# Chunk bounds by min/max trees, keys of eight heads in one DMA transpose, and a new instruction order

## The chip, the cores and the metric

The kernel runs on one core of a Trainium2 chip. The metric is the device time of one execution in microseconds (us); lower is better. The engines are named as the profile names them: PE (TensorE matmul; PEld its weight loads), DVE (VectorE), ACT (ScalarE), POOL (GpSimd), and SP, which here only issues DMAs. A name with a q (SPq) is an engine's instruction queue.

## The reference

Two stages. First a sparse causal attention over 4 batches, 8 heads, 768 positions and head size 64: every query keeps its 6 best chunks of 32 keys, ranked by an upper bound that comes from the minimum and maximum of each chunk. Then an MLP with an ELU over the 3072 tokens.

```python
k_min, k_max = min and max of k over each chunk of 32 keys       # 24 chunks per head
ub = sum over d of max(q*k_min, q*k_max), causal by chunk
top_chunks = argsort(ub)[..., -6:]
attn = softmax(where(key's chunk in top_chunks and key <= query, q @ k.T / 8, -1e9)) @ v
x = attn.transpose(0, 2, 1, 3).reshape(3072, 512)
h = x @ w_in                                                     # 512 -> 2048
out = where(h > 0, h, exp(min(h, 0)) - 1) @ w_out                # 2048 -> 512
```

## The kernel before

**Units.** The queries are cut into eight units of 384 tokens: unit 0 and unit 1 take the first half of batches 0 and 1 together (names with `p` and `s`), units 2 to 7 take batch and half (0,1), (1,1), (2,0), (2,1), (3,0), (3,1). For each unit the kernel prepares keys and queries (`prep_pair`, `prep`), selects chunks (`select`), attends (`attend_pair`, `attend`) and then runs the MLP (`mlp`). Below, H2 stands for one of the 16 first-layer blocks of unit 2 (L829, four matmuls of 128x384) and O2.1 for a quarter of token tile 1 of its second layer (L850, four matmuls of 128x512). The MLP of a unit is laid between the score (`sc`, L760) and value (`pv`, L811) matmuls of the next unit's attention on PE.

**Chunk bounds.** For batches 0 and 1 the bounds are reduced from transposed keys in PSUM (L362). For batches 2 and 3 `bounds_batch` loads the keys a second time with a chunk to each partition: 96 partitions (4 heads, 24 chunks), 32 keys of 64 numbers, in two loads of 16 keys (`kc`, one buffer). Each load gets two `tensor_reduce` on DVE, minimum and maximum (L481, out 96x64 from 96x1024 f32, read with a stride). Two small joins (`kj`, L485), a subtraction (`kz`), a PE transpose (`kw`, L492) and four copies (`kv`) bring the result to `kst`, which `select`'s matmul `ub` (L578) reads.

**Keys of batches 2 and 3.** `keys` casts 128 keys of eight heads into a `kt` buffer (`kb`), puts a one-hot row of the chunk beside them (`ky`), and SP issues two DMA transposes (`kd`, L463), one for heads 0 to 3 and one for heads 4 to 7, each 128x512 in bf16, into that group's own `lhs` buffer.

**From attention to the MLP.** The value matmuls of a head pair are followed by `rcp` (L622) and `on` (L624) on DVE, and for units 2 and up by a DMA transpose `xd` (L635) from SP. The first H block of a unit needs all four transposes of its unit.

**Order.** Nothing is scheduled at run time. A graph of operations is built, and a written-out string gives, three characters at a time, the engine and the operation; each engine runs its own instructions in the order of the string, and a second string gives the buffer slot of each new buffer. So an instruction that waits holds everything that stands behind it on its engine, and SP's and POOL's DMA issues wait in line as well. `fill` (L889) is a matmul on zeros that computes nothing.

Of the kernel before, what the change touches and what calls it, by code (L numbers as in the profile page):

```python
# [9 lines left out]
AOT = mybir.AluOpType  # L10
# [7 lines left out]
S = 768  # L18
D = 64
# [20 lines left out]
G0hD0nD01D00D0iD0jD0cG0eD06A0rS0tS0vS0xS0sS0uS0wS0yS0VS0WS0XS0YS0zS0BG0kG03G04D05PjNPjOPjPPjQPjR  # L40
P0DD09G0pG0lG0aG0bG0dD0oA02P0KA0LA0HP0MA0QP1oD0FD0ED0qP1uD0OD0ND0RP0TA0UP1kP1yP1jP1lA1mA1nG0mG0g
P11D13A15D12G0JP1pP1aD1ePjSPjTPjUPjVPjWP1hP18P1tP1qS0ZS0+S2fS2gS2hD0GD1iP1zA19P1vA1sA0IA1xA1wA10
G07G16S2iD1bG1gG0PG1fG0fG0AGmrGmsGmtD0CPjXPjYPjZPj-Pj+P1OP1AA1BGmuGmvGmwD0-P1DD1cP1EP1HP1SD1FP1I
G1dD1JP1RD1TD1GPk0Pk1Pk2Pk3P2oD1UP1ND2pD1KP2BD1PD1QD2DA1CP20P1YP1+D21D2qP1LA1rP1XP25P2aP29P26D22
D1ZD2bA2FA2sG2uG08D1-D2CD27G14S2IS2OS2vS2PS2QA1MA2HP1VA1WD28D2cS2RS2kPk4Pk5Pk6Pk7Pk8Pk9PkaPkbP23
PkcPkdPkePkfPkgPkhP2dD2eA24PmCA2GA17PkiPkjPkkPklP2wPmGP2JA2KD2MPkmPknPkoPmOPm-A2xA2LD2yG2rG2jGmx
D2NAmDAmHAm+G2SG2EP3lD3mD3nD3pD3oD2AAbeA0SA2zGmIDmEDmJDmFGn0D3qDn1D2tPmSPmWPmKPmyAmLAmXAmPGmYGmQ
D3rDmZD3uAmTDmUDmRDmVGmMPnuPnaPnmA3vP4FPn2AnvA3tA3sAnnGnwGnoDmNDnxDnpP41P4DPneAn3AmzA4GA4EAnbGn4
Dn5A42P4jA4kAnfP2XP3JP3HPniS32S5wS2mS2TS50S4+S2VS3fGmADncD2+DndPn6A3IAn7DmBPnLGngD2YD2ZDnhG2-G4H
Gn8P4lA3KG3LA4mA30P38PnqPnMPnED39Dn9AnrDnsD3aD3cD4nD3bG3dG31PnFP3+PnNAnjDnkDnlDntP3gP33PnGA34A36  # L50
G37G2lD3hG3jG3kG2nD3iA40G43D35P3wPnyPnOAnPD3ePnHS4ZD3xD3yD3zD3AD3BP3NA2UAnID3CG3DD3ES8hS4-S4YS7Q
S7US4XP4JP3MD3OP48P45P44D46P3QP4aA49A4bP4IA3RD3GD47D4cD4KPnzP3SP4OG3FP4uG2WP4eP4dP4sPnAD3PD4fD4g
D4LP4MA3TG3UP3WA4vA4tA4PP3VP4hA4ND4wP4xP4pP4yD3XD3YD4zP4oP3ZA3-P5fA5gG5iA5jP5rA5sP5ED4QG7RS7KS7O
ScMP4SP4RD4qD4AD4rD4iPnBD5FA5GD4TD4UP4BA4CP5xDnCP4VP5QP58D5uD5yA5BG5DG5IG5CA4WPoxP5JD5hD59D5zA5R
A5TD5SAoyGozG5HPo9AoaGobA5NA5tD5cD5aP5kD5mPodAoePnVAnWA7PGofG5UD5bDocD5lA5oDogDoAPohPo5Ao6S51G52
Go7G5ADnXPnZPnRPotD5LD5KDnYDo8ShqS55S7SS7IG5eG5nAnSGnTDnUA5vAouPo1Ao2An-GovDowD5MGo3Do4AoiSnKS57
S7NSazS7LGn+PoFA56AoGGojDo0PolAomPoBDokGoHDoIP5VD5WPoRPopPoXPoSPoYPp2Pp3G5pGonDooD5XAoqG5qGorAoC
GoDA5PD5YD5ZD5-D5+D60G5dP6gA62DoEA6hP6lP68A69P6mP6cA6dA6nDosPoTD7TSnJS53SnDS7JScKSaFDaHS7MSnQDaG
P66A67P6aP6iA6jD6kG61A6bPp4P6uA6vP6GA6HP6eA6fD6oG54PoJP6yP64A65A6zP6wA6xPoZAoKP6IP6LP6MP6pP6AA6J
A6BP6qDoLDoMP6CA6NG63G5OP7uP6EPoND6rD6sP74SaIA6DG6KA7vA6FAoOGoPSaBS6tA75P6YA6ZD6OP6PP79P7aP6QA7b  # L60
DaKDoQDbaDaMP76A77G78D6RPoUDaJP7AP7wA7xP70P7zD6SDaLDaNA71Pp5Dp6A7BP6UP6-P6WA6VP8cA6XS6TSp7SaTA6+
AoVPo-P7oP72P7sA73P7iP7mA7pA7nG7cP7dD8dG8fG8gG7CD7yDo+Sp1Sp0P7eP7kP7qP8iD7fD7gS7hA7jA7tA7rP85P7V
P8uP7DD8jD8eD7ZD7XA7lP7ED7FD7GD7+A7-A8ySayA8AP8BP8pA8qG8sS7HA89G8bA8CA8ED8mD8vD8wD8nP80A81A8aAaC
A8zA84AaAD86D7WD7YD87G8xG8oD8rD8DD88Db6ScOSaDPpsPpEPpgA82SaxSavSoWD8kDfMD8lGcNDaEAphG83GpiApFGpG
DpHPp8PpwPpAPpoAptAcLDpjGpuG8FDpvSatSauScEApBGpCDpDApxAcPGpyDpzAppGpqPpcApdAbdSbgDprPpIPpkDcRGpe
DpfAp9GpaDpbApJGpKAplGpmDpLPpMApNA8tP8GD8IPpQSffSfhPpYPq4PpUAq5DpnPq8PqkGpOGb5Sb8ScGSbfApRGq6GpS
Gb9SbcD8KD8HD8JSawSbbShoApZPq0Aq1ApVDpTD8LD8MA8PPq9PqlDpPPqmDq7D8QGp-Dp+Dq2Dq3G8NP91A92P8ZPafAag
A8-D8OGpWDpXPqaP93A94G95P97P8RA8SP9tP96P9rP8VA9uA98P8XA8YPqbP8TP8+A9sA90PbmPqnDcYDqcScJSb7ScFDcQ
# [870 lines left out]
```

## Time and profile before

| | before |
|---|---|
| time, median of 3 runs | 303.69 us (300.88 to 304.95) |
| the profiled execution | 303.33 us, of it the span in the profile 301.6 us |
| busy: PE, DVE, ACT, POOL | 273.8, 230.6, 205.6, 127.7 us |
| mean granted TensorE clock | 0.983 |
| `fill` matmuls run | 40 |
| instructions | 6849 |

Busy time is the union of an engine's instructions. In views by windows each row is a stretch of the span: its length, then the busy time of each engine with the number of its instructions that start there, the clock granted to PE (1.00 is full), the busy share of the DMA engines and what they moved. In rows of the timeline the first number is the start, the second the duration, and the brackets hold how long the engine had been idle and what ended that.

### The profile page before, as it was taken

The numbers are of one execution on the slowest core, as the hardware profiler recorded it, in microseconds if no ns is written. First come the engines' busy times: TensorE is split into PE (matmuls) and PEld (weight loads), VectorE is DVE, ScalarE is ACT, GpSimd is POOL, SyncE is SP. The second block draws the span as 40 slices with busy tenths as digits, with TensorE's granted clock in tenths as the row PEclk, the third lists the DMA queues.
The fourth block names the chain that finished last, engine by engine and source line by source line (L and its number), as shares of the span: only waits on it lengthen the run. The fifth ranks groups of instructions, "written<-read, shape, count | busy, mean of one in ns | idle before, by whom it ended". The sixth has DMA issues, their size and how long they took to land.

```text
span 301.6 us, 6849 instructions
## 1 busy us (share of the span) xinstructions
PE 273.8 (91%) x2408; PEld 164.6 (55%) x2436; DVE 230.6 (76%) x622; ACT 205.6 (68%) x455; POOL 127.7 (42%) x254
## 2 busy tenths in 40 slices
PE   6779799999996879999699889999969999999994
PEld 4456454775464745567256446567535646665641
DVE  5673989799989878858899989784998679622740
ACT  3556792878496877689368929977766959891720
POOL 8862356448533357531366404402444515400510
PEclk9999999999999979999689999999999999999999
DMA  6999999999750599999697424823420230013002
GB/s 157 193 181 206 199 206 183 214 215 220 181 152 20 171 240 153 181 257 143 147 205 157 105 56 103 175 55 93 129 42 4 62 96 0 27 38 110 24 0 105
DMA packets 107347, 39.25 MB, mean 130 GB/s; under 512 B 98864, under 2 KB 102960, under 8 KB 107312
## 3 DMA queue, kind: packets, MB, share of 16 engines
q1 hardware_dynamic: 103216, 34.52, 56.3%
q0 software_dynamic: 3696, 4.19, 8.0%
q8 instruction: 19, 0.31, 0.5%
q14 instruction: 16, 0.13, 0.2%
q10 hardware_dynamic: 400, 0.10, 0.1%
HBM read 30.41 MB, written 6.29 MB: 122 GB/s over the span
## 4 chain that ended last, share of the span: by engine, by line
PE 50%; DVE 25%; DMA 11%; ACT 5%; issue 4%; POOL 2%; SPq 1%; POOLq 0%; ACTq 0%; DVEq 0%
PE bank L850 17%; PE bank L829 14%; DVE km L481 9%; PE bank L760 6%; DVE gT L842 5%; PE bank L811 4%; DMA kc<-in_k_dram 4%; DMA xt<-on 3%; DMA f<-in_v_dram 2%; PE bank L578 2%; DVE on L624 2%; PE bank L397 2%; ACT e L836 1%; DVE thr L597 1%; PE bank L529 1%
## 5 line engine op out<-in xcount | busy, mean ns | idle before, releaser
L829 PE MATMUL bank<-xt,w_in_sb 128*128 128x384 bf16 x512 | 95.4, 336 | 8.6 <-DMA xt<-on 4.6
L850 PE MATMUL bank<-w_out_sb,gT 128*128 128x512 bf16 x357 | 89.3, 379 | 2.3 <-DVE gT L842 0.7
L838 POOL TENSOR_SCALAR m<-e 128x384 f32<-128x384 f32 x96 | 49.2, 525 | 80.4 <-ACT e L836 67.0
L836 ACT ACTIVATE e<-bank 128x384 f32<-128x384 f32 x128 | 58.2, 491 | 28.5 <-PE bank L829 24.5
L829 PEld LDWEIGHTS <-w_in_sb 128*128 128x128 bf16 x512 | 50.8, 100 | 46.3 <-issue 17.3
L775 ACT ACTIVATE pt<-bank 128x384 bf16<-128x384 f32 (+1 forms) x144 | 66.5, 544 | 7.7 <-PE bank L760 5.9
L842 DVE SCALAR_TENSOR_TENSOR gT<-bank,m 128x384 bf16<-128x384 f32 x128 | 65.9, 549 | 4.9 <-POOL m L838 3.5
L850 PEld LDWEIGHTS <-gT 128*128 128x128 bf16 x384 | 36.1, 97 | 39.6 <-DVE gT L842 2.7
L760 PE MATMUL bank<-rhs,lhs 96*128 96x384 bf16 (+2 forms) x240 | 42.7, 293 | 1.8 <-DVE on L624 1.7
L792 POOL TENSOR_TENSOR pt<-pt,tri 128x256 bf16<-128x256 bf16 (+1 forms) x23 | 20.1, 884 | 31.7 <-ACT pt L779 18.0
L481 DVE TENSOR_REDUCE km<-kc 96x64 f32<-96x1024 f32 x16 | 30.3, 1909 | 2.4 <-DMA kc<-in_k_dram 2.3
L760 PEld LDWEIGHTS <-lhs 96*128 96x128 bf16 x240 | 21.4, 97 | 13.8 <-issue 0.5
L316 POOL CAST rhs<-qt 64x384 bf16<-64x384 f32 x26 | 13.7, 530 | 27.8 <-DVE qt L316 15.4
L811 PE MATMUL bank<-vext,pt 128*128 128x65 bf16 x576 | 23.2, 193 | 1.5 <-DVE pt L792 1.2
L811 PEld LDWEIGHTS <-pt 128*128 128x128 bf16 x576 | 21.5, 97 | 5.2 <-DVE pt L792 1.9
L314 ACT ACTIVATE o<-bank 128x512 f32<-128x512 f32 x12 | 7.2, 596 | 23.8 <-PE bank L850 23.6
L624 DVE TENSOR_TENSOR on<-bank,rcp 128x384 bf16<-128x384 f32 (+1 forms) x40 | 19.7, 500 | 1.1
L362 DVE TENSOR_REDUCE kst<-bank 128x12 f32<-128x384 f32 x32 | 16.9, 547 | 3.8 <-ACT kt L314 2.5
L622 DVE RECIPROCAL rcp<-bank 128x6 f32<-128x6 f32 (+1 forms) x40 | 7.2, 185 | 14.7 <-PE bank L811 11.9
L316 DVE COPY o<-bank 128x512 f32<-128x512 f32 x12 | 8.3, 690 | 13.1 <-PE bank L850 12.9
L838 DVE TENSOR_SCALAR m<-e 128x384 f32<-128x384 f32 x32 | 12.7, 403 | 5.8 <-ACT e L836 5.7
L792 DVE TENSOR_TENSOR pt<-pt,tri 128x512 bf16<-128x512 bf16 (+1 forms) x25 | 10.8, 443 | 6.3 <-ACT pt L779 4.2
(95 smaller groups left out, 315.7 us busy)
## 6 DMA issues: line engine op xcount, KB each, us to landing
f<-in_v_dram SPq DMA_DIRECT2D x22, 256.0 KB, 4.8
out_dram<-o SPq DMA_DIRECT2D x22, 256.0 KB, 2.5
f<-in_q_dram SPq DMA_DIRECT2D x18, 256.0 KB, 4.0
f<-in_k_dram SPq DMA_DIRECT2D x18, 256.0 KB, 4.7
kc<-in_k_dram SPq DMA_DIRECT2D x8, 384.0 KB, 3.9
w_out_sb<-in_moe_w_out_dram POOLq DMA_DIRECT2D x4, 512.0 KB, 21.4
f<-in_k_dram SPq DMA_DIRECT2D x6, 192.0 KB, 5.4
f<-in_q_dram SPq DMA_DIRECT2D x6, 192.0 KB, 7.3
```

Of the source, the lines that this page charges most:

```text
L316: eng[e].tensor_copy(out=dst, in_=src)
L481: nc.vector.tensor_reduce(out=ap(km)[0:96, y, w], in_=ap(kc)[0:96].rearrange("p (w d) -> p d w", d=D), axis=AX.X, op=op), reads=[(kc, 0)], ...
L624: g.op("on" + tag, (DVE,), lambda e: nc.vector.tensor_tensor(out=ap(on)[:, 0:nt].rearrange("p q h d -> p h q d"), in0=view()[:, :, :, 0:D] ...
L760: nc.tensor.matmul(ap(banks[hd])[:, o + pc:o + pc + wd], lhsT=ap(ls)[0:96, pr, hd, P * kb:P * (kb + 1)], rhs=ap(rs)[0:96, hd, c0 - HS * h: ...
L775: lambda e, hd=hd, pt=pt, banks=banks, wtot=wtot: nc.scalar.activation(out=ap(pt)[:, hd, PAD:PAD + wtot], in_=ap(banks[hd])[:, 0:wtot], fu ...
L792: eng[e].tensor_tensor(out=view, in0=view, in1=tri[:, 64:64 + P].rearrange("p (a b w) -> p a b w", a=1, b=1) .to_broadcast([P, 2, len(dg), ...
L811: nc.tensor.matmul(view()[:, hd, qi, :], lhsT=ap(pt)[:, hd, P * qi + off:P * qi + off + P], rhs=ap(vx[b])[:, kb, 2 * r + hd, :], start=(kb ...
L829: nc.tensor.matmul(ap(bank)[:, 0:HS], lhsT=w_in_sb[:, kk, P * fc:P * (fc + 1)], rhs=ap(xT[i, kk]), start=(kk == 0), stop=(kk == NKK - 1))
L836: g.op(f"e{i}.{fc}", (ACT,), lambda e, eb=eb, bank=bank: nc.scalar.activation(out=ap(eb), in_=ap(bank)[:, 0:HS], func=AF.Exp), reads=[(ban ...
L838: g.op(f"m{i}.{fc}", (POOL, DVE), lambda e, eb=eb, mb=mb: eng[e].tensor_scalar(out=ap(mb), in0=ap(eb), scalar1=-1.0, scalar2=1.0, op0=AOT. ...
L842: nc.vector.scalar_tensor_tensor(out=ap(gt), in0=ap(bank)[:, 0:HS], scalar=0.0, in1=ap(mb), op0=AOT.max, op1=AOT.min),
L850: nc.tensor.matmul(ap(bank), lhsT=ap(gts[fc])[:, P * tt:P * (tt + 1)], rhs=w_out_sb[:, fc, :], start=(fc == 0), stop=(fc == NFC - 1))
```

## The change

Four edits of the program text, and a new order.

1. `bounds_batch`: each `tensor_reduce` over 16 keys becomes four `tensor_tensor` of 512, 256, 128 and 64 numbers. The first step of the minimum writes a new buffer `kn`; the maximum folds `kc` in place. Each tree is two operations of the order: `a` (the 512 wide step) and `b` (the other three).
2. `keys`: one DMA transpose of 128x1024 for all eight heads in place of two of 128x512. `lhs` has one buffer per batch for all four head pairs (2 buffers, each twice as large; before 4).
3. The zeroed columns of `kt` now also take columns 96 to 128 of the first four heads, and readers wait for that memset (`kp`).
4. The order and the buffer slots are written anew; `gT` has 17 buffers in place of 20; 33 `fill` matmuls run in place of 40.

```diff
+    def apl(b, G):
+        return ap(b)[:, 2 * G:2 * G + 2]
+    slots("kn", [P, 512], F32)
-    slots("lhs", [P, 2, 2, S], BF16)
+    slots("lhs", [P, NPAIR, 2, S], BF16)
...
-            for G in range(NG):
-                lb = lhs[b, G]
-                g.op(f"kd{tag}{x}{G}", (SP,), lambda e, kp=kp, x=x, lb=lb, G=G: eng[e].dma_start_transpose(
-                    out=ap(lb)[:, :, :, HS * h + P * x:HS * h + P * (x + 1)].rearrange("p a b s -> p (a b) s"),
-                    in_=ap(kp)[:, 4 * G:4 * G + 4].rearrange("p h c -> p (h c)")),
-                    reads=[(kp, 0), (kp, 1), (fixed, "kq")], writes=[(lb, (h, "d", x))], dma=True)
+            lb = lhs[b]
+            g.op(f"kd{tag}{x}", (SP,), lambda e, kp=kp, x=x, lb=lb: eng[e].dma_start_transpose(
+                out=ap(lb)[:, :, :, HS * h + P * x:HS * h + P * (x + 1)].rearrange("p a b s -> p (a b) s"),
+                in_=ap(kp).rearrange("p h c -> p (h c)")),
+                reads=[(kp, 0), (kp, 1), (fixed, "kq"), (fixed, "kp")], writes=[(lb, (h, "d", x))], dma=True)
...
-                for w, op in enumerate((AOT.min, AOT.max)):
-                    g.op(("kmin", "kmax")[w] + f"c{tag}{y}", (DVE,), lambda e, w=w, op=op, kc=kc, y=y, km=km:
-                         nc.vector.tensor_reduce(
-                             out=ap(km)[0:96, y, w], in_=ap(kc)[0:96].rearrange("p (w d) -> p d w", d=D),
-                             axis=AX.X, op=op), reads=[(kc, 0)], writes=[(km, (w, y))])
+                t = Buf("kn")
+                g.op(f"kminc{tag}{y}a", (DVE,), lambda e, t=t, kc=kc: nc.vector.tensor_tensor(
+                    out=ap(t)[0:96], in0=ap(kc)[0:96, 0:512], in1=ap(kc)[0:96, 512:1024], op=AOT.min),
+                    reads=[(kc, 0)], writes=[(t, 0)])
+                g.op(f"kmaxc{tag}{y}a", (DVE,), lambda e, kc=kc: nc.vector.tensor_tensor(
+                    out=ap(kc)[0:96, 0:512], in0=ap(kc)[0:96, 0:512], in1=ap(kc)[0:96, 512:1024], op=AOT.max),
+                    writes=[(kc, 0)])
+                for w, op, src in ((0, AOT.min, t), (1, AOT.max, kc)):
+                    def rest(e, w=w, op=op, src=src, y=y, km=km):
+                        for n in (256, 128, 64):
+                            nc.vector.tensor_tensor(
+                                out=ap(src)[0:96, 0:n] if n > 64 else ap(km)[0:96, y, w], in0=ap(src)[0:96, 0:n],
+                                in1=ap(src)[0:96, n:2 * n], op=op)
+                    g.op(("kmin", "kmax")[w] + f"c{tag}{y}b", (DVE,), rest,
+                         writes=[(src, 0), (km, (w, y))])
```

The two order strings, decoded, at the places that the prediction speaks of (xN: N in a row; `...` leaves out):

```
PE before: fills ahead of the first H0: 33
PE after:  fills ahead of the first H0: 28, of them 18 in a row
PE before, last values of unit 2 to H2:  pv01r3x2 qT113 qT112 qT110 H2
PE after:                                pv01r3x2 qT113 qT112 qT110 H2
PE before, unit 3 to H3:  pv11r3x2 qT210 H3x10 kw21 H3x2 ub20
PE after:                 pv11r3x2 qT210 qT213 O2.1 kw21 H3x7 ub20
PE before, unit 4 to H4:  pv20r3x2 ub21 O3.2x2 H4
PE after:                 pv20r3x2 ub21 O3.0 O3.2x3 H4
PE before, inside H5:     H5x13 kw31 H5x2 ub30
PE after:                 H5x10 kw31 H5x5 ub30

DVE before, unit 2 tail:  rcp011 kminc201 on011 kj200 kz20 ...
DVE after:                rcp011 kmaxc201b oe1.1 on011 kminc201b rcp012 on012 ...
DVE before, unit 3 tail:  kminc210 rcp112 qr202 on112 qt200 qr200 rcp113 on113 kv2011 kmaxc210
DVE after:                rcp112 kminc211a on112 kminc211b rcp113 on113 kmaxc211a kmaxc211b kj210 kj211 kz21
DVE before, into H5:      kminc311 kmaxc311 ... qr301 g5.5 g5.10 kminc310 g5.9 ... kmaxc310
DVE after:                kminc311b ... kminc310a kminc310b qr301 kmaxc310a kj310 kmaxc310b g5.7

SP before, first issues:  one k load on ACT; 11 k and q loads, then the first v load
SP after:                 five k loads on ACT; ldk ldq ldq ldq ldq ldv ...
SP before, around kc:     ldc201 ldv201 xd010 xd011 out1.2.0 ldc210
SP after:                 ldc201 xd010 ldv200 ldq111 ldk111 out1.0.0 ldc210 out1.1.0 out1.2.0 xd011

operations by engine, before and after:
  m (L838): DVE 32, POOL 96       -> DVE 21, POOL 107
  qr (L336, L338): DVE 15, ACT 13 -> DVE 8, ACT 20
  qa (L316 and L314): DVE 11, ACT 19, POOL 26 -> DVE 6, ACT 21, POOL 29
  ky: DVE 7, ACT 2, POOL 3 -> DVE 1, ACT 5, POOL 6
  oe: DVE 12, ACT 12 -> DVE 10, ACT 14
  kd (SP): 24 -> 12
```

More of the change, by code (lines that the diff above doesn't have):

```diff
@@ L45 @@
[L45 to L56, printed above, removed]
@@ L117 @@
-63072265gi3210026171123435064771212246571456104775604012023130010572120011126c06201e3422123001b5
-722020f21025411017920024522102a74dh120
-"""
-BUFS = dict(f=11, kc=1, km=1, kt=5, lhs=4, vext=2, rhs0=4, rhs1=5, kst=2, qt=5, qr=4, ubT=1, thr=2,
-            selb=2, selT=2, pt=8, rcp=3, on=4, xt=7, e=3, m=3, gT=20, o=3)
+01234050123456760127308400953111a220015401311622342131625400610135322120576576576576576576576135
+721124222043014630561140163052680300000111512421620732021311024210052007104103052a62792118609021
@@ L123 @@
+21329250d111306a22000221cf712046120
+"""
+BUFS = dict(f=11, kc=1, kn=1, km=1, kt=5, lhs=2, vext=2, rhs0=4, rhs1=5, kst=2, qt=5, qr=4, ubT=1, thr=2,
+            selb=2, selT=2, pt=8, rcp=3, on=4, xt=7, e=3, m=3, gT=17, o=3)
 NG = 2
@@ L403, in prep_pair @@
         bank = Buf("bank")
-        kst, lb = ks[b], lhs[b, G]
+        kst, lb = ks[b], lhs[b]
         g.op("kT" + tag, (PE,), tr(bank, kf), reads=[(f, G) for f in kf] + [(fixed, "idf")],
@@ L520, in prep @@
                 load_v(f"{b}{h}{x}", b, 3 * h + x, 0, P)
-        lb, kst = lhs[b, G], ks[b]
+        lb, kst = lhs[b], ks[b]
         if b < 2 and pr == 0:
@@ L543, in prep @@
             put("kt" + tag, flat, lambda: ap(bank)[:, 0:HS],
-                (ACT, DVE), [(bank, 0)], [(kt, 0)])
+                (ACT, DVE), [(bank, 0), (fixed, "kp")], [(kt, 0)])
             for hd, half in enumerate((lo, hi)):
-                put(f"ka{hd}{tag}", lambda hd=hd: ap(lb)[lo, pr, hd, ts], lambda half=half: flat()[half],
-                    (POOL, DVE, ACT), [(kt, 0)], [(lb, (h, x, hd, pr)) for x in range(2)])
+                put(f"ka{hd}{tag}", lambda hd=hd: ap(lb)[lo, r, hd, ts], lambda half=half: flat()[half],
+                    (POOL, DVE, ACT), [(kt, 0)], [(lb, (h, x, hd, r)) for x in range(2)])
         elif r == 0:
@@ L699, in cols @@
                     return ap(pt)[:, hd, col:col + P]
-                ls = lhs[b, G]
+                ls = lhs[b]
                 for hd in range(2):
@@ L748, in attend @@
         seg = {}
-        ls, rs = lhs[b, G], rhs[b, h + 1, r]
+        ls, rs = lhs[b], rhs[b, h + 1, r]
         for si, segs in enumerate(steps[h]):
```

167 lines of the change are left out of this document (90 added, 77 removed).

## The prediction

> **What bounds the kernel now.** I read the page's totals first, then the windows by stage, then PE's rows with idle time in front of them, and last what DVE and SP did at those moments.
>
> ```profile
> span 301.6 us, 6849 instructions
> ...
> PE 273.8 (91%) x2408; PEld 164.6 (55%) x2436; DVE 230.6 (76%) x622; ACT 205.6 (68%) x455; POOL 127.7 (42%) x254
> ```
>
> ```profile
> 90.00:110.00 20.00, 15.21 (x164) 10.34 (x164) 17.02 (x37) 15.86 (x37) 6.88 (x13) 0.95 0.52 125
> 140.00:152.00 12.00, 8.85 (x73) 5.07 (x70) 10.77 (x19) 6.11 (x14) 4.89 (x10) 0.73 0.73 160
> 170.00:182.00 12.00, 10.19 (x106) 5.27 (x107) 10.83 (x44) 5.43 (x12) 2.64 (x4) 1.00 0.29 68
> 182.00:210.00 28.00, 27.61 (x262) 17.33 (x265) 21.13 (x43) 23.83 (x53) 8.51 (x15) 1.00 0.50 108
> 210.00:231.00 21.00, 18.63 (x136) 10.50 (x135) 19.66 (x46) 12.89 (x35) 9.83 (x20) 1.00 0.27 65
> ```
>
> PE is the bound: 273.8 of 301.6 us. The change takes no work from it but seven fills, so it can gain only where PE stands or is granted less than the full clock. From 182 to 210 PE is busy 27.6 of 28 us: nothing is to be had there. Four stretches have holes: 90 to 110 (20 - 15.21 = 4.8 us idle), 140 to 152 (3.15), 170 to 182 (1.8), 210 to 231 (2.4), together 12.1 us. In the first two the clock falls as well: 0.05 x 20 = 1.0 us and 0.27 x 12 = 3.2 us of lost full-speed time. So the middle holds some 16 us at most. In these stretches DVE is at 82 to 94%, and each is where the late batches' chunk bounds are made. What ended the idle time:
>
> ```profile
> 97.25 0.32 PE L760 MATMUL bank<-rhs,lhs 96*128 96x384 bf16 x1 [1.71 <-DVE on L624]
> 107.15 4.15 PE L829 MATMUL bank<-xt,w_in_sb 128*128 128x384 bf16 x15 [2.17 <-DMA xt<-on]
> 146.70 0.48 PE L829 MATMUL bank<-xt,w_in_sb 128*128 128x384 bf16 x1 [1.78 <-DMA xt<-on]
> 220.71 3.41 PE L829 MATMUL bank<-xt,w_in_sb 128*128 128x384 bf16 x20 [1.73 <-DVE gT L842]
> ```
>
> ```profile
> 94.90 1.83 DVE L481 TENSOR_REDUCE km<-kc 96x64 f32<-96x1024 f32 x1
> 96.66 0.54 DVE L624 TENSOR_TENSOR on<-bank,rcp 128x384 bf16<-128x384 f32 x1
> ```
>
> The 1.71 us is the plainest: the normalisation `on` stood for 1.8 us behind a reduce, and PE waited for its bank. The chain of waits (start, duration, what) says the same of 210 us: two reduces in a row, then two more between evacuations, then PE waits for gT. Its first row gives the price of a quarter of O, 0.86 us for four matmuls.
>
> ```profile
> 204.93 0.86 PE bank L850 x4
> ...
> 210.93 3.67 DVE km L481 x2
> 214.62 3.66 DMA kc<-in_k_dram
> 218.29 1.90 DVE km L481
> 220.19 1.39 DVE gT L842 x3
> ```
>
> **The trees.** Their price comes from DVE operations on two f32 inputs in SBUF:
>
> ```profile
> L481 DVE TENSOR_REDUCE km<-kc 96x64 f32<-96x1024 f32 x16 | 30.3, 1909 | 2.4 <-DMA kc<-in_k_dram 2.3
> L485 DVE TENSOR_TENSOR km<-km x8: 205/212/702, 94.2 to 223.9; 96x64 f32<-96x64 f32 x8
> L485 DVE TENSOR_TENSOR km<-km 96x64 f32<-96x64 f32 x8 | 2.4, 306 | 0.0
> L602 DVE TENSOR_TENSOR selb<-ubT,thr 128x576 bf16<-128x576 f32 x4 | 3.1, 777 | 0.1
> ```
>
> From 212 ns at 64 wide (median) to 777 at 576 wide is 1.10 ns for each number: 706, 424, 283 and 212 ns for the four steps, 1.63 us a tree against 1.91. Sixteen trees save 16 x 0.28 = 4.5 us of DVE. But L485 has a mean of 306 and a longest of 702: 94 ns over its median. If each of the 64 steps pays that too, 6.0 us come back and the trees cost 1.5 us more than the reduces. So the trees' DVE time changes by -4.5 to +1.5 us; I take -1.5, the middle. The worth lies elsewhere: a reduce pair holds `kc` for 3.8 us; its successor's last reader is done after 0.71 + 0.71 + 0.92 = 2.3 us, and the longest stretch that evacuations wait behind is 0.9 us if pieces are interleaved. What stood beside the slow L485:
>
> ```profile
> 93.01 1.78 POOL L792 TENSOR_TENSOR pt<-pt,tri 128x512 bf16<-128x512 bf16 x2 [1.34 <-ACT pt L775]
> 93.23 1.02 DVE L316 COPY kt<-onehot 128x256 bf16<-128x256 bf16 x1
> 94.17 0.70 DVE L485 TENSOR_TENSOR km<-km 96x64 f32<-96x64 f32 x1
> ```
>
> A POOL product ran, and the L485 beside it took over three times its median. The Trainium skill, "SBUF — State Buffer", section "Who interferes with whom", has a rule that speaks against this change: a DVE instruction with two SBUF inputs contends with a POOL instruction that reads SBUF, and the loser waits for the whole instruction, while a `tensor_reduce` never contends. By that rule all 64 steps become exposed where none of the 16 reduces was; the trace agrees in that this one stretched and that the reduces' mean of 1909 ns shows no such tail. What it would do here is a rival below, priced by L485's rows.
>
> **Work moved off DVE.** Eleven `m` leave it, the largest part:
>
> ```profile
> L838 DVE TENSOR_SCALAR m<-e 128x384 f32<-128x384 f32 x32 | 12.7, 403 | 5.8 <-ACT e L836 5.7
> L838 POOL TENSOR_SCALAR m<-e 128x384 f32<-128x384 f32 x96 | 49.2, 525 | 80.4 <-ACT e L836 67.0
> ```
>
> That is 11 x 0.403 = 4.4 us. With seven `qr`, five `qa`, six `ky` and a few others less six `kv` more, some 20 pieces at about the same 0.4 us (an estimate from this row), 8 us more go, and with the trees DVE comes to about 217. POOL gets 11 x 0.525 = 5.8 us and a few copies (135), ACT about 10 (215). All three stay below PE, and POOL has the room: it stood 67 us waiting for `e` at this line. Off the path this is worth nothing by itself; it is why I let the holes close in part.
>
> **One transpose for eight heads.**
>
> ```profile
> L463 SPq DMA_TRANSPOSE lhs<-kt x24: 1190/1260/2150, 115.2 to 217.5; - x24
> xt<-on SPq DMA_TRANSPOSE x24, 2.8
> lhs<-kt SPq DMA_TRANSPOSE x24, 3.5
> 89.79 8.63 SPq L635 DMA_TRANSPOSE xt<-on  x2
> 241.73 1.16 PE bank L578 x25
> ```
>
> Three blocks land in 2.8 us, four in 3.5: 0.7 a block, so eight in about 6.3. SP saves 12 issues x 1.26 = 15 us of its queue, if an issue costs the same for twice the size; none if it doubles. Nothing waits for it either way: the last of before is issued at 217.5, and the scores of its unit cannot start before the selection that begins at 241.73. I cost it at nothing; if that cover of 20 us went, it would be 2.8 us for each of four halves. More telling is what SP stands behind: 8.63 us for two `xd`, with a `kc` load right behind them. In the new order that load stands ahead of the second `xd`.
>
> **The start and the fills.**
>
> ```profile
> 7.26 4.14 SPq L301 DMA_DIRECT2D f<-in_v_dram  x4
> 10.18 6.13 DMA f<-in_v_dram
> 0.00:25.00 25.00, 18.59 (x177) 12.54 (x179) 16.31 (x45) 12.33 (x25) 19.38 (x63) 1.00 1.04 180
> L889 PE MATMUL bank<-zeros 128*128 128x256 bf16 x40 | 7.8, 289 | 4.9 <-DVE zeros L244 2.0 <-DVE kst L362 1.0 <-DVE on L624 0.8
> ```
>
> The chain runs over the v loads to 16.3 us. With k on ACT's queue the first v load is sixth on SP, issued some 4 us sooner, but the DMA engines are full (share 1.04), so bytes set the pace. I take -0.5; bounds -3 and +2, the latter because four matmuls that need POOL's `identb` now stand in front of PE's first transposes. Seven fills (7.8 / 40 = 0.2 us each) stood where PE waited anyway: 0 to -1.4, taken 0; if they kept the clock, the loss is bounded by the 3.2 us seen at 140.
>
> **The sum**, from the execution's own 303.33 us:
> - 90 to 110: of the 1.71 us and the small waits around it most goes, -1.5 (0 to -2.6, all but the next). The 2.17 us stay: behind the last values of unit 2 stand the same three transposes.
> - 140 to 152: between the last values and H3 now lie one more `qT` (0.3), a quarter of O (0.86) and `kw21`: -1.2 (0 to -2.2); with shorter idle most of the lost clock comes back, -2 (0 to -3.2).
> - 170 to 182: two more quarters of O ahead of H4, -0.5 (0 to -1.8).
> - 210 to 231: the four reduces no longer stand in pairs before gT, -1.3 (0 to -2.4).
> - start -0.5.
> - New waits that a new order brings: +0.7 (0 to +10, above SP's largest stand).
>
> -1.5 - 1.2 - 2 - 0.5 - 1.3 - 0.5 + 0.7 = -6.3: **297.0 us**, 2.2% under the median of 303.69, which the profiled execution matches within 0.4 us. About 2% is what a measurement of this kernel can tell from no change, the shown runs lying 1.3% apart; that bound is 297.6, so the forecast lies next to it.
>
> **The rivals.**
> *Holes only move.* The stretched trees (+1.5 us of DVE, by L485's mean) leave `on` and gT as late as before, or PE finds its covers elsewhere: the hole of 2.17 us stays, and so do most others, only the start and the clock give something. 303.3 - 0.5 - 1.5 = 301.3, with half the holes 299. For it: DVE stays at 72%, and the new order still puts pieces of 0.7 to 1.6 us between `rcp112` and `rcp113`. Against: the pieces are shorter everywhere. The rule of "SBUF — State Buffer" in the Trainium skill would bring this case about; L485's 702 ns is all that the trace shows of it. Chance 0.38.
> *All holes close.* -12.1 and -4.2 from the middle would give 287; without the 2.17 us at H2, and with four fifths of the other 14.1, it is 292. For it: DVE's relief. Against: the same in-order queues. Chance 0.12.
> *Slower: DVE stands at a kc load.* The trees are more closely laced with `rcp` and `on` than the reduces were (`kminc211a` between `rcp112` and `on112`), and `kw21` now stands ahead of H3 on PE. If SP, in line behind an `xd` or an output, brings a kc load late, DVE stands with the normalisation behind it, then `xd`, then PE. Price: SP's 8.63 us less the 2.3 us that DVE waits for kc now, 6.3 us a place; two of the four places give 303.3 + 12.6 - 3 = 312.9. It decides from a kc load that SP reaches over 2 us after DVE reaches its piece. Against: the loads stand earlier in SP's line. Chance 0.10.
>
> **How the numbers follow.** The forecast has 0.40, the others 0.38, 0.12 and 0.10. It lies just beyond the bound, and I count 0.37 of it as faster and 0.03 as within 2%: faster 0.37 + 0.12 = 0.49, same 0.38 + 0.03 = 0.41, slower 0.10. The forecast's own range is 294 to 298.5; with "holes only move" and the near side of "all holes close", and some room for the runs' own 1.3%, it is 290.5 to 304. That leaves out the slow case and the far end of the fast one.
>
> **What would show it.** Right: no row L481, 64 tensor_tensors of 0.2 to 0.8 us from kc and kn with a sum of 26 to 33 us; DVE near 217, POOL 135; 12 `kd` landing in 5 to 7 us; no wait of PE for `on` over 1 us; the clock over 0.9 everywhere. Wrong: PE waiting for xt or km for over 3 us at an H burst, DVE idle before a kc piece, tree steps of twice their size, or H0 starting after 25 us.

## The result and the profile after

The changed kernel takes 289.76 us (median of 4 runs, 288.53 to 290.75) against 302.84 us (4 runs, 300.88 to 304.95): ratio 0.957, interval 0.949 to 0.964. The prediction was 297.0 us with a range of 290.5 to 304. The direction was right, the gain was twice the forecast, and the time lies just below the range. The profiled execution took 289.5 us. A few executions that lay over 1.5% above the fastest of the same kernel are left out of all times and ratios.

The page's totals after the change:

```profile
span 287.8 us, 6917 instructions
...
PE 271.3 (94%) x2429; PEld 164.3 (57%) x2429; DVE 218.6 (76%) x637; ACT 213.4 (74%) x472; POOL 140.8 (49%) x271
```

PE stands for 287.8 - 271.3 = 16.5 us where it stood for 27.8: 11.3 of the 13.8 us that the span lost. The other 2.5 us are PE's busy time, where the seven fills and the lower clock had been; some matmul records are missing before (357 of 384 at L850), so this part is rough. The windows of the changed kernel (length, then busy time of PE, PEld, DVE, ACT, POOL, then granted clock, DMA share, GB/s):

```profile
0.00:25.00 25.00, 20.62 (x173) 13.86 (x174) 13.32 (x41) 12.59 (x26) 17.64 (x57) 1.00 1.18 194
25.00:75.00 50.00, 48.42 (x482) 30.48 (x482) 41.53 (x129) 40.06 (x88) 29.38 (x58) 1.00 1.03 197
90.00:110.00 20.00, 17.72 (x212) 11.95 (x210) 19.05 (x44) 18.34 (x43) 13.20 (x22) 1.00 0.97 198
140.00:160.00 20.00, 18.69 (x141) 10.73 (x140) 17.91 (x49) 17.43 (x40) 14.62 (x25) 1.00 0.61 149
```

A stretch of the kernel before that the prediction had not looked at:

```profile
25.00:75.00 50.00, 46.36 (x465) 29.87 (x474) 41.22 (x125) 36.05 (x77) 24.93 (x47) 1.00 1.17 206
```

The clock is full in all of these windows. In 90 to 110 PE went from 15.21 to 17.72 of 20 us, and 25 to 75, which the prediction did not count among the stretches with holes, went from 46.36 to 48.42. Rows of PE with idle time in front of them, after (start, duration, what, in brackets the idle time and what ended it):

```profile
102.19 4.87 PE L844 MATMUL bank<-xt,w_in_sb 128*128 128x384 bf16 x29 [1.78 <-DMA xt<-on]
...
139.32 0.30 PE L507 MATMUL bank<-ident_f,km 96*128 96x96 f32 x1 [1.62 <-DVE km L503]
139.46 4.71 PE L844 MATMUL bank<-xt,w_in_sb 128*128 128x384 bf16 x28
```

The hole ahead of H2 has stayed (2.17, now 1.78). The one ahead of H3 is now a wait for `km`. The 1.71 us for `on` ahead of it has no row of its size left, nor has the 1.73 us for gT at 220. Where the time came from, by the start of the first H block of each unit in the two traces (us of the span):

| stage | before | after | change | forecast |
|---|---|---|---|---|
| start to H0 | 24.9 | 24.6 | -0.3 | -0.5 |
| H0 to H1 | 39.4 | 38.2 | -1.2 | 0 |
| H1 to H2 | 39.7 | 37.0 | -2.7 | -1.5 |
| H2 to H4 | 75.6 | 69.7 | -5.9 | -3.7 |
| H4 to H5 | 34.0 | 34.3 | +0.3 | 0 |
| H5 to H6 | 31.2 | 28.5 | -2.8 | -1.3 |
| H6 to the end | 56.8 | 55.5 | -1.2 | 0 |

With +0.7 for new waits, in no stage of its own, the forecast column gives -6.3; the traces give -13.8. Every stretch behind H1 that was named gained more than its term, and two stages that had no term gained 1.2 us each. How much of the -5.9 hangs on the clock of this one execution is shown below (a_again).

### The profile page after: what moved, and what is told of

The parts are those of the page before. It is cut to its first block, busy times and chain, and to the rows that moved or that the text cites. A ratio compares the mean times of both kernels' runs of the same rounds, so it can differ in the third digit from the quotient of the medians.

```text
span 287.8 us, 6917 instructions
## 1 busy us (share of the span) xinstructions
PE 271.3 (94%) x2429; PEld 164.3 (57%) x2429; DVE 218.6 (76%) x637; ACT 213.4 (74%) x472; POOL 140.8 (49%) x271
## 4 chain that ended last, share of the span: by engine, by line
PE 65%; DVE 20%; ACT 5%; DMA 4%; issue 3%; POOL 2%; DVEq 0%; POOLq 0%; ACTq 0%
PE bank L865 22%; PE bank L844 20%; PE bank L775 8%; PE bank L826 5%; DVE gT L857 4%; PE bank L403 2%; PE bank L593 2%; POOL m L853 2%; DVE thr L612 2%; DMA f<-in_q_dram 2%; DVE on L639 2%; PE bank L544 2%; ACT pt L790 1%; DVE kst L368 1%; DVE kn L494 1%
## 5 line engine op out<-in xcount | busy, mean ns | idle before, releaser
L865 PE MATMUL bank<-w_out_sb,gT 128*128 128x512 bf16 x384 | 92.3, 379 | 0.3 <-DVE gT L857 0.2
L844 PE MATMUL bank<-xt,w_in_sb 128*128 128x384 bf16 x512 | 89.5, 326 | 3.3 <-DMA xt<-on 1.8
L853 POOL TENSOR_SCALAR m<-e 128x384 f32<-128x384 f32 x107 | 56.2, 536 | 58.0 <-ACT e L851 47.7
L844 PEld LDWEIGHTS <-w_in_sb 128*128 128x128 bf16 x512 | 49.3, 98 | 38.9 <-issue 7.3
L807 POOL TENSOR_TENSOR pt<-pt,tri 128x256 bf16<-128x256 bf16 (+1 forms) x24 | 22.7, 958 | 28.3 <-ACT pt L794 18.7
L323 POOL CAST rhs<-qt 64x384 bf16<-64x384 f32 x29 | 15.1, 526 | 23.7 <-ACT qt L321 16.5
L794 ACT ACTIVATE pt<-bank 128x512 bf16<-128x512 f32 x24 | 14.6, 617 | 3.0 <-PE bank L775 2.9
L321 ACT ACTIVATE rhs<-selT 32x384 bf16<-32x384 bf16 (+1 forms) x12 | 8.2, 682 | 9.1 <-DVE selT L621 8.9
L544 PE MATMUL bank<-ident_f,f 128*128 128x128 f32 x96 | 14.3, 276 | 0.6 <-DVE on L639 0.5
L321 ACT ACTIVATE rhs<-qt 64x384 bf16<-64x384 f32 x21 | 10.6, 519 | 3.4 <-DVE qt L323 3.2
```

The source lines that it names most:

```text
L321: nc.scalar.activation(out=dst, in_=src, func=AF.Copy)
L544: nc.tensor.transpose(ap(bk)[:, P * j:P * (j + 1)], ap(src[j])[:, P * r:P * (r + 1)], ident_f)
L807: eng[e].tensor_tensor(out=view, in0=view, in1=tri[:, 64:64 + P].rearrange("p (a b w) -> p a b w", a=1, b=1) .to_broadcast([P, 2, len(dg), ...
L844: nc.tensor.matmul(ap(bank)[:, 0:HS], lhsT=w_in_sb[:, kk, P * fc:P * (fc + 1)], rhs=ap(xT[i, kk]), start=(kk == 0), stop=(kk == NKK - 1))
L853: g.op(f"m{i}.{fc}", (POOL, DVE), lambda e, eb=eb, mb=mb: eng[e].tensor_scalar(out=ap(mb), in0=ap(eb), scalar1=-1.0, scalar2=1.0, op0=AOT. ...
L865: nc.tensor.matmul(ap(bank), lhsT=ap(gts[fc])[:, P * tt:P * (tt + 1)], rhs=w_out_sb[:, fc, :], start=(fc == 0), stop=(fc == NFC - 1))
```

## The experiments

Runs that start from the kernel before have labels with b, those from the changed kernel with a. Two theories lead. LIMITS: the gain comes from what is taken out of DVE's and SP's lines (long reduces, half of the `kd` issues). ORDER: it comes from the new positions and engine choices. For the kernel before there are two more, BLOCK (the reduces hold up what stands behind them on DVE) and CLOCK (the time is lost to PE's clock). All ratios are to the kernel before in runs on the same chip. Edits are given in short form.

### The changed kernel again

> The changed kernel once more, as the yardstick for the runs beside it. Every theory: 288 to 291 us, a ratio of 0.95 to 0.965 to the kernel before.

290.66 us, ratio 0.964 (0.961 to 0.966). Against 0.957 in the first set, this shows how far two sets of one kernel lie apart: 2 us by the ratios. Where PE's waits and stage times of a profile are compared below, a_again is the partner.

Its profiled execution (292.04 us) waited 1.80 us for xt at H2, the one of the section above (289.5 us) 1.78. Behind that wait the two ran at different clocks, first a_again, then the execution above:

```profile
104.20:107.60 3.40, 3.40 (x12) 1.59 (x11) 2.45 (x8) 2.58 (x7) 1.68 (x5) 0.50 1.27 222
```

```profile
103.90:107.30 3.40, 3.40 (x28) 1.86 (x34) 3.40 (x11) 3.38 (x9) 2.31 (x6) 1.00 1.32 226
```

From H2 to H4 a_again takes 72.0 us and the other 69.7; in all other stages the two agree within 0.3. So 3.6 of the 5.9 us gained there are common to both, and 2.3 go with the 3.4 us at half clock, which the kernel before had as well (0.50 from 108.0 to 111.4 us).

### Reduces in place of the trees, in the new order

```diff
 kminc..a: - tensor_tensor(kn, kc[0:512], kc[512:1024], min)   + tensor_reduce(km of min, kc, min)
 kmaxc..a: - tensor_tensor(kc, kc[0:512], kc[512:1024], max)   + nothing
 kminc..b: - three steps                                       + nothing
 kmaxc..b: - three steps                                       + tensor_reduce(km of max, kc, max)
```

(The minima of some heads are written over those of the heads before them; the number and size of the instructions are those of the kernel before.)

> The new order with the reduces put back: the minimum stands where the first step of its tree stood, the maximum where the last steps of its tree stood; all else as changed. Theory ORDER (the gain is the new order; the trees bring nothing, since their 64 steps take 32.4 us of DVE against 30.3 for the reduces): within 1.5 us of the changed kernel, 288 to 291. Theory TREES (short pieces let evacuations through, and kc comes free sooner): at least 4 us over it, 294 or more, with PE again waiting 1 us and more for on and gT.

294.06 us, 0.974 (0.970 to 0.979): 3.4 us slower than a_again. The trees as pieces in this order are worth about that. In its profile PE waits 3.4 us for gT and 3.2 for xt, against 2.6 and 2.3 in a_again.

### Two transposes of four heads, in the new order

```diff
-dma_start_transpose(out=lhs[all 8 heads], in_=kp)
+[dma_start_transpose(out=lhs[group G], in_=kp[:, 4*G:4*G+4]) for G in range(2)]
```

> The new order with two DMA transposes per key tile again, issued one behind the other in the place of the one. ORDER: within 1 us of the changed kernel, since the transposes have over 20 us to spare. Theory KEYS (SP's queue was the brake, and 12 issues less free it): 3 us or more over it, with kc loads and xd issued later by some 1.3 us for each issue in front of them.

295.29 us, 0.980 (0.977 to 0.982): 4.6 us slower than a_again. PE's row and SP's queue, first of a_again, then of a_two_kd:

```profile
138.59 0.87 PE L544 MATMUL bank<-ident_f,f 128*128 128x128 f32 x6 [0.19 <-DMA f<-in_q_dram]
...
126.62 1.37 SPq L468 DMA_TRANSPOSE lhs<-kt  x1
...
132.03 0.57 SPq L305 DMA_DIRECT2D f<-in_q_dram  x1
```

```profile
141.99 1.54 PE L544 MATMUL bank<-ident_f,f 128*128 128x128 f32 x6 [5.25 <-DMA f<-in_q_dram]
...
124.09 5.19 SPq L468 DMA_TRANSPOSE lhs<-kt  x4
129.33 0.58 SPq L305 DMA_DIRECT2D f<-in_v_dram  x1
129.95 4.03 SPq L468 DMA_TRANSPOSE lhs<-kt  x2
...
136.37 0.57 SPq L305 DMA_DIRECT2D f<-in_q_dram  x1
```

Nothing waits for a `kd`. What waits is a q load that stands behind them in SP's line: it is issued 4.3 us later, and PE stands 5.25 us where it stood 0.19. Behind this wait PE then runs at half clock, 15 matmuls where a_again starts 28 at 1.00:

```profile
142.00:146.30 4.30, 4.30 (x15) 2.70 (x16) 3.13 (x12) 3.25 (x8) 0.00 (x0) 0.50 0.79 169
```

From H2 to H4 a_two_kd takes 75.8 us, as much as the kernel before (75.6; a_again 72.0).

### Trees, or the merged transpose, in the old order

```diff
# b_trees                                     # b_kd
-nc.vector.tensor_reduce(km, kc, op)          -kd..0: transpose of heads 0 to 3
+four tensor_tensor: 512, 256, 128, 64 wide   +kd..: whichever comes first turns all eight heads
 in place of each reduce, at its place        +the other issues nothing
```

> The old order with the trees in the place of the reduces, four steps in a row in each reduce's place (the extra buffer lies over two constants that are no longer read by then). ORDER: within 1.5 us of the kernel before, 301 to 304, since a row of four steps holds DVE for as long as a reduce. TREES: 3 us or more faster, 300 or less.

> The old order with one key transpose for eight heads, issued where the first of the two stood. LIMITS: PE waits only 0.8 us for a q load at 144 us, so SP is not what holds it: 0 to 1.5 us gained, 300.5 to 302. KEYS (SP's queue is the brake everywhere): 3 to 5 us gained, as two transposes cost the new order 4.6.

b_trees: 305.75 us, 1.011 (1.006 to 1.017), slower by 3.5 us. b_kd: 300.96 us, 0.998 (0.995 to 1.000), 0.5 faster, which is not clear of the noise. So neither brings its worth along: the same trees cost 3.5 us in the one order, where they stand in rows of four, and save 3.4 in the other, in pieces.

### Both undone in the new order

The edits of a_reduce and a_two_kd together.

> The new order with the reduces and with two key transposes (as in the two runs before, both undone; some minima again overwrite those of the heads before, which changes values and no instruction). If the two parts add up: 290.7 + 3.4 + 4.6 = 298.7, and the order with its engine choices is worth 3 us. LIMITS (the one waits in the shade of the other): 295.5 to 297.

296.37 us, 0.981 (0.977 to 0.984). With both undone 5 of the 11 us of a_again are still there: that much is due to the positions and the engine choices. By stages, the gains from H0 to H2 and from H5 to H6 are all kept (38.2, 36.8 and 28.5 us; a_again 38.2, 37.0 and 28.5), and nothing is left of the one from H2 to H4 (75.8; before 75.6). The two parts do not add: 3.4 + 4.6 = 8.0 would have given 298.7. With two transposes the trees are worth no more than the noise (0.981 against 0.980 in a_two_kd); that PE then stands for q anyway would explain it.

### BLOCK: the reduces nearly removed, in the old order, and the tree steps, in the new one

```diff
# b_light: minima and maxima over 2 of 16 keys
-in_=kc[0:96]                +in_=kc[0:96, 0:2*D]
# b_light_kd: the same, with the edit of b_kd
# a_light: of each tree, only 64-wide steps are left
-for n in (256, 128, 64):    +for n in (64,):
```

> The old order with reduces over 2 of the 16 keys of each load (the bounds leave out the other 14): about 28 us less on DVE, at the same places. Theory BLOCK (the holes of PE from 90 to 231 us, and the clock lost behind them, come from the time for which DVE stands in these reduces, whatever the order): 291 to 295, most of the gain of the change. ORDER with COVERS (the holes come from too little PE work between a unit's last values and its first H block): 298 to 303, the holes of 2.17 and 1.78 us at H2 and H3 stay.

> The old order with the light reduces (2 of the 16 keys of each load, the others left out of the bounds) and with one key transpose for eight heads. LIMITS: with DVE relieved SP's line is next (PE waited 3.8 us for a q load with the light reduces), so the merged transpose now pays 2.5 to 4 us: 290 to 291.5. If it pays no more here than in the old order by itself, there are not two limits that take turns.

> The new order with only the 64 wide step of each tree (it compares 2 of the 16 keys of a load, so the bounds leave out the other 14; the same instructions follow). DVE loses about 28 us of work. If DVE's work on the bounds still held PE up, the time falls by 3 us or more, to 286 or less; ORDER says that what is left of PE's idle time is the waits for xt and the start, and that it falls by 0 to 2 us.

b_light: 293.93 us, 0.973 (0.969 to 0.978), 8 us faster. b_light_kd: 293.35 us, 0.971 (0.966 to 0.975), no further gain that the noise lets see, where LIMITS wanted 2.5 to 4. a_light: 288.49 us, 0.956 (0.952 to 0.959), 2.2 faster than a_again. So the reduces' DVE time is worth 8 us in the old order, and the trees' only 2 in the new one. In the old order what then ends last is a q load that stands behind two `xd` on SP, which the merged transpose barely moves (issued at 136.8 us in b_light and 136.6 in b_light_kd; PE of b_light_kd):

```profile
141.11 0.69 PE L532 MATMUL bank<-ident_f,f 128*128 128x128 f32 x2 [3.19 <-DMA f<-in_q_dram]
```

### CLOCK, and the place of two reduces, in the old order

```diff
# b_fills: 16 zero matmuls ahead of the first H block of units 2 and 3
+for _ in range(LEAD.pop(i, 0)):
+    nc.tensor.matmul(ap(bank)[:, 0:256], lhsT=zeros[:, 0:P], rhs=zeros, start=True, stop=True)
# b_moved: two reduces behind the normalisations that stood behind them
+MOVES = (("kminc201", "on011"), ("kminc210", "on113"))
```

> The old order with 16 matmuls on zeros ahead of H2 and of H3, in the time in which PE waited for xt (they write the bank that the H block then overwrites). Theory CLOCK (some 4 us of the loss are the lower granted clock behind these two waits): the clock stays above 0.95 in 95 to 155 us, and 1.5 to 4 us are gained, 299 to 301.5. If the clock does not hang on these waits: no gain, or up to 2 us lost.

> The old order with two reduces moved on DVE: the one that stood between rcp011 and on011 goes behind on011, the one ahead of rcp112 goes behind on113, so that no bound stands in front of the last normalisations of units 2 and 3. BLOCK: the wait of 1.71 us for on goes and H3 comes about 2 us sooner, with more clock: 298 to 301. ORDER with COVERS: under 1.5 us gained.

b_fills: 300.99 us, 0.998 (0.995 to 1.001). The windows of the kernel before, and of b_fills:

```profile
140.00:155.00 15.00, 11.85 (x90) 6.78 (x87) 13.77 (x22) 7.63 (x17) 6.83 (x13) 0.77 0.85 172
```

```profile
140.00:155.00 15.00, 11.15 (x82) 6.76 (x86) 13.40 (x24) 7.34 (x18) 7.34 (x14) 1.00 0.87 169
...
152.23 0.81 PE L832 MATMUL bank<-xt,w_in_sb 128*128 128x384 bf16 x4 [1.56 <-DVE gT L845]
```

The clock is back from 0.77 to 1.00 and PE only arrives earlier at a wait for gT; some 1 us at most is gained. b_moved: 303.19 us, 1.005 (1.002 to 1.008). It lets `on` go first, and PE waits for gT instead, 3.03 us:

```profile
155.69 1.44 PE L830 MATMUL bank<-xt,w_in_sb 128*128 128x384 bf16 x4 [3.03 <-DVE gT L843]
```

CLOCK falls for the old order. There DVE itself is busy 13.77 of the 15 us between 140 and 155. In these two runs neither a faster PE nor another place for a reduce helped; taking work off DVE did (b_light).

### The covers ahead of H3 and H4, taken away

```diff
+MOVES = (('o2.1.3', 'h3.9'), ('oe2.1', 'o2.1.3'), ('out2.1.0', 'oe2.1'),
+         ('o3.2.2', 'h4.4'), ('o3.2.3', 'o3.2.2'), ('oe3.2', 'o3.2.3'))
```

Each pair puts the first operation behind the second: a quarter of O2.1 behind the third H3 block, two quarters of O3.2 behind the fourth H4 block, each with its evacuation.

> The new order with the covers ahead of H3 and H4 taken away: a quarter of O2.1 goes behind the third H3 block, two quarters of O3.2 behind the fourth H4 block, as they stood later in the old order. COVERS (my terms of 140 to 152 and 170 to 182 us): PE waits for xt 0.8 us more at H3 and 1.5 to 1.9 us more at H4, and the time rises by 1.5 to 2.5 us. If DVE or SP sets the pace there, PE makes the wait good later and the time rises by under 0.7 us.

296.91 us, 0.982 (0.977 to 0.987): 6.3 us slower than a_again. Three quarters of O at 0.86 us make 2.6. The rows of a_uncover:

```profile
141.88 0.42 PE L508 MATMUL bank<-ident_f,km 96*128 96x96 f32 x1 [2.76 <-DVE km L504]
142.09 4.05 PE L845 MATMUL bank<-xt,w_in_sb 128*128 128x384 bf16 x12
...
176.88 2.27 PE L845 MATMUL bank<-xt,w_in_sb 128*128 128x384 bf16 x13 [2.01 <-DMA xt<-on]
```

The windows of a_uncover (the granted clock is the figure ahead of the last two), then one of a_again:

```profile
143.00:144.00 1.00, 1.00 (x4) 0.45 (x3) 0.04 (x1) 0.38 (x1) 0.00 (x0) 0.50 1.13 324
...
146.00:147.00 1.00, 0.78 (x3) 0.39 (x3) 0.00 (x0) 0.00 (x0) 0.00 (x0) 0.50 0.00 0
147.00:148.00 1.00, 1.00 (x5) 0.41 (x4) 0.18 (x1) 0.00 (x0) 0.00 (x0) 0.71 0.00 0
```

```profile
143.00:144.00 1.00, 1.00 (x8) 0.61 (x7) 0.75 (x3) 1.00 (x4) 0.52 (x1) 1.00 1.05 311
```

Without its cover the wait for `km` is 2.76 us (a_again: 1.53), and `kw21` with H3 behind it starts at the same 141.9 us as in a_again, with the quarter still to do. Then PE runs at half clock until some way into 147: 4 matmuls in a microsecond where a_again has 8, and 12 of them in 4.05 us against 28 in 4.71 in the changed kernel. About 5.4 us at 0.50 are up to 2.7 us that no price of a cover contains. In the first H4 block PE stands 2.01 us for xt. H3 to H4 is 2.1 us longer than in a_again, H4 to H5 3.2.

### Positions against engine choices

216 operations stand on another engine in the new order. b_engines takes these engines into the old order, a_engines the old engines into the new order.

```diff
-o.emit({"P": PE, "A": ACT, ...}[order[j]])
+o.emit(ENGINE.get(o.name, {"P": PE, "A": ACT, ...}[order[j]]))
```

> The old order, position by position, with the new order's choice of engine for 216 operations (DVE gives 99 of them away and takes 69, so it is relieved by some 10 us; the constants at the start and the loads keep their engines). Theory LIMITS (between H2 and H4 of the old order DVE's work sets the pace, and close behind it SP's line of loads and key transposes): 297 to 300, two thirds of what the reduces' 28 us gave. ORDER (engine choices pay only where they were placed together with the positions): within 2 us of the kernel before, 300 to 304.

> The new order, position by position, with the old order's choice of engine for 216 operations (DVE gets some 10 us more). If positions and engine choices are one fit: 10 us or more slower than the changed kernel, as the old order was 28 us slower with the new choices. If DVE's load alone counts: 3 to 6 us slower.

b_engines: 331.3 us, 1.096 (1.090 to 1.101). a_engines: 308.56 us, 1.022 (1.016 to 1.027). With the new engines DVE has 220 us of work in place of 231, and yet the kernel is 30 us slower, where both theories had put it at 297 to 304 us. DVE's waits (what waited for what, us in total, times, longest) before, then of b_engines:

```profile
DVE gT L842 <- POOL m L838: 3.5, 8, 1.0
```

```profile
DVE gT L843 <- POOL m L839: 23.0, 21, 3.5
```

An `m` on POOL that stands behind other work there holds DVE, and all that stands behind gT on it, 23 us in all. This is the largest of its new waits; how much of the 30 us it carries was not tried. The old engines in the new order cost 18 us. A relief of DVE in busy time was worth nothing by itself here: positions and engines are one fit.

### The fills, `kw21`, and a shorter tree

```diff
# a_nofill: the 33 fills issue nothing      # a_kw: kw21 behind h3.2, kv2110 behind it
# a_best: as a_kw, and after the first step of each tree one reduce of 512
-for n in (256, 128, 64): tensor_tensor     +tensor_reduce(km, src[0:96, 0:512])
```

> The new order without its 33 matmuls on zeros. All of them stand in the first 25 us, where PE waits anyway. My price of nothing: within 1 us of the changed kernel; the granted clock may fall in the first 30 us, which would cost up to 3 us.

> The new order with the transpose kw21 of the bounds behind two H3 blocks in the place ahead of them (and its first copy behind it): PE waited 1.5 to 1.6 us for it with H3's inputs there. If this wait is on the path: 0.8 to 1.5 us gained, 289 to 290. If DVE is the limit there: within 0.5 us.

> kw21 moved as in the run beside it, and each tree halved: the 512 wide step stays, one reduce over the remaining 512 numbers does the rest (about 0.69 + 0.96 = 1.65 us by half of a reduce's 1.91, against 2.02 measured for a tree; fewer steps with two SBUF inputs). By the 2 us that taking nearly all of the trees' work away gave, at most 0.5 us more than the run beside it: 288.5 to 290.

a_nofill: 290.93 us, 0.962 (0.958 to 0.967), no difference from a_again, though its clock is 0.85 in the first 25 us:

```profile
0.00:25.00 25.00, 17.04 (x152) 11.09 (x153) 15.79 (x44) 13.81 (x28) 17.86 (x57) 0.85 1.10 184
```

a_kw: 289.08 us, 0.959 (0.954 to 0.964): the wait of 1.6 us for `km` is gone, and 0.33 and 0.62 us for xt stand there instead. a_best: 289.08 us, 0.957 (0.952 to 0.962). These are the best times among the runs of the experiments that compute all of the reference, but not clear of a_again or of the first set.

### The tree steps by themselves

A kernel that only runs the disputed steps, each alone and then beside POOL's `m` (attention and MLP are left out). It ran once.

> No attention and no MLP, the output is filled with a constant: the steps by themselves, in stages. DVE's 512 wide minimum alone, then its maximum beside POOL's 128x384 tensor_scalar, the same for the 64 wide step, then reduces alone and beside POOL, then POOL alone. If two SBUF inputs contend with POOL (the rule of "SBUF — State Buffer" in the Trainium skill): alone 0.69 and 0.21 us, beside POOL each stretched, up to a POOL operation of 0.5 us more, and POOL's stretched too; the reduce 1.9 us in both. If not: the same durations in both stages, and the trees' long tails come from something else.

Each row gives shortest, median and longest in ns:

```profile
L78 DVE TENSOR_TENSOR t<-kc x16: 675/678/689, 4.9 to 13.9; 96x512 f32<-96x512 f32 x16
L82 DVE TENSOR_TENSOR t<-kc x24: 674/982/985, 14.5 to 34.9; 96x512 f32<-96x512 f32 x24
L83 POOL TENSOR_SCALAR m<-e x24: 505/939/1008, 15.3 to 36.3; 128x384 f32<-128x384 f32 x24
L87 DVE TENSOR_TENSOR r<-kc x16: 205/210/222, 37.0 to 39.0; 96x64 f32<-96x64 f32 x16
L92 DVE TENSOR_TENSOR r<-kc x40: 203/548/551, 39.2 to 52.6; 96x64 f32<-96x64 f32 x40
L98 DVE TENSOR_REDUCE r<-kc x8: 1849/1850/1860, 53.1 to 65.5; 96x64 f32<-96x1024 f32 x8
L103 DVE TENSOR_REDUCE r<-kc x8: 1851/1881/1887, 67.3 to 80.0; 96x64 f32<-96x1024 f32 x8
L111 POOL TENSOR_SCALAR m<-e x16: 510/511/514, 82.7 to 89.9; 128x384 f32<-128x384 f32 x16
```

Beside POOL a 512-wide step goes from 678 to 982 ns and POOL's `m` from 511 to 939; a 64-wide one goes from 210 to 548; a reduce goes from 1850 to 1881. By the rule of the Trainium skill that the prediction named ("SBUF — State Buffer", "Who interferes with whom"), steps with two SBUF inputs contend with POOL's reads and a `tensor_reduce` does not; these rows agree with both halves.

## Why the prediction was right, and where it was not

**Right in kind.** PE was the bound, only the seven fills were taken from it, and the gain came for the most part out of its idle time, 27.8 to 16.5 us. The hole at H2 stayed (1.78), the start gave 0.3 of 0.5, the fills were worth nothing, and DVE, ACT and POOL came to 218.6, 213.4 and 140.8 where 217, 215 and 135 were forecast. That DVE's sum came so near is luck: the trees added 2.1 us where -1.5 was taken, and the work moved off took 14.1 where 12.4 was. Of the four signs against it none appeared, except that some tree steps were stretched. One reading was off: DVE's share in the windows shown is 85 to 94%, not 82 to 94.

**The ceiling.** "Four stretches have holes", together 12.1 us, was the first step that failed. PE's idle time was 27.8 us, 6.4 of it in the first 25; so 9.3 us lay elsewhere and were not looked at: 3.6 from 25 to 75, 4.5 from 276 on (nearly all behind PE's last matmul), the rest in short gaps. PE's idle time from 25 to 75 fell by 2 us. Of the 7.5 us between forecast and traces, the stages without a term make 2.1, the three named ones behind H1 4.9, and the rest is the +0.7 that did not come, less 0.2 at the start.

**"140 to 152" and "170 to 182".** Together -3.7, measured -5.9 from H2 to H4, or -3.6 in a_again, which like the kernel before ran 3.4 us at half clock behind H2; the forecast had no term for that spell. That -3.6 is so near is in part luck, as the next step shows. The covers were priced at their own 0.86 us a quarter. a_uncover shows what stands behind them: about 6 us for three quarters, because the longer idle time ahead of H3 is followed by some 5 us at half clock, and because what comes late at H4 is handed on. A term for the clock was right for the new order, where PE has work to do at once (a_again's 3.4 us at half clock go with 2.3 us), and wrong for the old one (b_fills: 1 us at most); its size of -2 was not measured by itself.

**The merged transpose.** "I cost it at nothing" is the second step that failed, at 4.6 us in the new order. With two transposes nothing is gained from H2 to H4 (75.8 us; before 75.6), so the terms there, which name only covers and clock, had left out what they rest on. I asked who waits for the `kd` and found 20 us of cover; I did not ask what stands behind it on SP, where the q and kc loads of the next batch do. Its landing was misjudged as well: 3.5 us for eight heads, not 6.3 (12 landings in 5 to 7 us were a sign of being right).

```profile
xt<-on SPq DMA_TRANSPOSE x24, 2.5
lhs<-kt SPq DMA_TRANSPOSE x12, 3.5
```

**The trees.** Their sum after the change:

```profile
L494 DVE TENSOR_TENSOR kn<-kn 96x256 f32<-96x256 f32 (+1 forms) x16 | 7.7, 480 | 0.3
L494 DVE TENSOR_TENSOR kc<-kc 96x256 f32<-96x256 f32 (+1 forms) x16 | 6.7, 418 | 0.4
L485 DVE TENSOR_TENSOR kn<-kc 96x512 f32<-96x512 f32 x8 | 6.5, 818 | 0.1
L488 DVE TENSOR_TENSOR kc<-kc 96x512 f32<-96x512 f32 x8 | 6.1, 758 | 0.1
L494 DVE TENSOR_TENSOR km<-kn 96x64 f32<-96x64 f32 x8 | 2.8, 349 | 0.3
L494 DVE TENSOR_TENSOR km<-kc 96x64 f32<-96x64 f32 x8 | 2.6, 328 | 0.3
```

32.4 us, against 30.3 for the reduces: +2.1, past the upper bound of +1.5 (taken: -1.5). The base price was right (706 ns worked out, median 689), and the tail is contention with POOL: 17 of the 64 steps took over 0.1 us longer than the shortest of their size, all of them beside a POOL instruction, and none of the 31 without one did. The trace before showed it twice, not once: a second L485, at 154.2 us, took 0.48 us beside an `m`. That the worth lies "elsewhere", in shorter pieces between which the evacuations get through, held in the new order: 3.4 us, where the pieces are interleaved. In the old one, where they are not, they lose 3.5, though the steps take 31.1 us of DVE there; 3.2 of it come between H3 and H4 (38.4 us, before 35.2). That the rows of four are the reason is not shown.

**"90 to 110" and "210 to 231"**, -1.5 and -1.3, gave -2.7 and -2.8 by stage (H1 to H2, H5 to H6), both just past the far end of their bounds (-2.6 and -2.4). I stood at the middle of these bounds. a_both keeps both gains, so in the new order they come from positions and engine choices; in the old one b_light gains 2.7 and 2.3 there, so the reduces held these stretches up. **"New waits"** of +0.7 are real (the one for `km` at H3), but worth little: without it (a_kw) H2 to H4 takes 69.4 us, with it 69.7, both at full clock.

**The rivals.** "All holes close" at 292 came nearest, with 0.12. "Holes only move" describes edits made alone in the old order (b_trees, b_kd, b_fills, b_moved), not the change. "DVE stands at a kc load" did not happen; the trouble it named, SP's line, is what the merged transpose removes.

**Open.** How the 11 to 14 us divide is no single sum, since the parts are worth different amounts in each other's presence: 3.4 and 4.6 alone, 5.7 together. Which of the new positions and engine choices make the remaining 5 us, from H0 to H2 and from H5 to H6 above all, was not tried; the covers lie between H2 and H5.

## What to carry to other kernels

Price a DMA by what stands behind it in its queue, not only by who waits for its landing; and price a piece of covering work by taking it away in thought, with the clock that the longer idle time then costs. Count all idle time of the engine that bounds before naming the stretches that can gain. In a hand-ordered kernel a part tried alone in the old order says little: the trees lost 3.5 us there and gained as much in an order made for them. Compare the clock of two profiles before their stages: here 2.3 us between two executions of one kernel went with it.

## What the hardware showed beyond expectation

An eight-block DMA transpose landed in 3.5 us in the new order and 4.4 in the old (b_kd), a four-block one in 2.6 (a_two_kd) and 3.5: four more blocks cost 0.9 us, where 0.7 us a block had been worked out. Its issue held SP 1.4 us (median; 1.8 in b_kd), a four-block one 1.3. A 64-wide DVE step on two SBUF inputs beside POOL went from 210 to 548 ns, so the relative loss is largest for the smallest steps. And after an idle time of 2.76 us PE ran at a granted clock of 0.50 for some 5 us, where it stayed at 1.00 after one of 1.53 at the same place in a_again. The length of the wait alone does not decide: after 1.80 us at H2 the clock was 0.50 for 3.4 us in a_again, after 1.78 it stayed at 1.00 in the changed kernel.
